# A multi-head attention block on one core: x transposed by DMA instead of by TensorE

## The chip, the cores and the metric

The kernel runs on one core of a Trainium2 chip. A core has five engines with queues of their own: TensorE (PE, with a row of its own in the profile for weight loads, PEld), VectorE (DVE), ScalarE (ACT), GpSimd (POOL) and SyncE (SP). Each engine executes its instructions in the order in which they stand in its queue; an instruction that has to wait holds up all that stand behind it. Transfers are issued from the queues of SP, ACT and POOL and are moved by 16 DMA engines that all queues share. The metric is the device time of one execution in microseconds (us).

## The reference

```
B, S, D, H = 1, 2048, 448, 16
qkv = (x @ wqkv).reshape(B, S, 3, H, 28).transpose(2, 0, 3, 1, 4)
scores = einsum("bhqd,bhkd->bhqk", q, k) * 28 ** -0.5
o = einsum("bhqk,bhkd->bhqd", softmax(scores), v)
out = o.transpose(0, 2, 1, 3).reshape(B, S, D) @ wo
```

All inputs and the output are bfloat16. x is 2048 x 448, wqkv is 448 x 1344, wo is 448 x 448.

## The kernel before, in words

The 16 heads are worked on in four groups of four (g = 0 to 3). A head of 28 numbers takes one of four bands of 32 partitions. The 2048 queries are cut into four chunks of 512 (c) and the 2048 keys into 16 tiles of 128. A pair of group and chunk is a set; there are 16 sets, one after another. Within a set, PE multiplies a tile of keys KA with a chunk of queries QP and leaves scores in PSUM. ACT takes most of them through the exponential (line 928, tiles of 128 x 1024, into `pt`). DVE does the others by an exponential of its own in integers (line 943, into `I`), of which shifted copies J are added by DVE (line 1014) or by an accumulating DMA that POOL issues (line 990). PE then multiplies pt, I and J with three scaled versions of V into bank `o` (line 1073). The sums are normalised (line 1123) and multiplied with WO.

K, Q and V are projections of x. A contraction runs over partitions, so PE needs x with its 448 columns on partitions: that is `XT`, for each of four blocks of 512 rows. The columns are cut in CC = 4 chunks of CK = 112, so that the weights lie as 112 x 4 x columns. x is loaded as it is (`load_x`, line 140, tiles `xs`): partition p gets rows 16p to 16p + 15, and block b takes the four of them from 4b on. `xt_job` transposes it: 16 PE transposes of 128 x 112 a block (line 621), half of them copied from PSUM into XT by ACT (line 629), half by DVE (line 627). Afterwards the xs tiles hold the normalised outputs. The rows of a block are therefore not neighbours in x, and the output is written with the same rearrangement (`out_perm`).

The start of the kernel is this. SP and ACT each issue half of x and one of the two small weight pieces of group 0 for K (tile `o_sb`, called G1) and for Q (tile `rr`, called G0); SP then issues the three full weights `WRAW` (W2 for V, W0 for Q, W1 for K). ACT loads its function table (line 160). PE runs ten matmuls on zeros (line 643), then transposes and projections. For group 0, `k_first` projects the keys of one block (line 298), ACT squares them (line 324), PE sums the squares over a head with `blockK` (line 409), DVE takes the maximum `kp` (line 414). When all four blocks have their maximum, DVE works out `kmt`, `kroot` and `su` (lines 418, 420, 496), which every score of the first set needs: su is the offset that keeps the exponential in range. `q_job` and `qn_first` do the same for the queries of chunk 0 (`z`, line 457, and the norm, line 487).

The operand QP has the queries and, in the free rows of a band, the offsets. SP fills constant rows by 16 small transfers (line 198, from a `pt` tile), then writes z (line 661) and su (line 502) into QP of chunk 0. Until that is there, a score is computed by two matmuls, one with z and one with su; the function `wide` decides which form is emitted.

The order on the engines is fixed when the kernel is built. A planner steps through time with a duration for every operation and takes, for each engine, the ready operation with the best priority; transfers from DRAM enter with a due time that is written down in a table (`evt[n] = (t, "DMA")`), which holds due times and isn't measured. It emits zero matmuls (line 762) where PE would otherwise stand still. On the chip the queues keep the planned order, and semaphores make each instruction wait until its data are there. Transfers share eight semaphores in turn: where a transfer takes one that an earlier transfer still holds, its issue waits until that one has landed.

Of the kernel before, what the change touches and what calls it, by code (L numbers as in the profile page):

```python
# [7 lines left out]
ACT = mybir.ActivationFunctionType  # L8
ALU = mybir.AluOpType
AX = mybir.AxisListType  # L10
BF16 = mybir.dt.bfloat16
# [28 lines left out]
def kernel(  # L40
# [7 lines left out]
    nc = tc.nc  # L48
    P = 128
    _, S, D = x.shape  # L50
    H = 16
    Dh = D // H
    HP = 32
    G = 4
    HG = 4
    CC = 4
    CK = D // CC
    QW = 512
    NQC = S // QW
    NKT = S // P  # L60
# [6 lines left out]
    WPAD = 4  # L67
    XB = 4
    NXB = NKT // XB
# [26 lines left out]

    x2 = x[0]
    out2 = out[0]
    out_perm = out2.rearrange("(p t) d -> p t d", t=NKT)

    const = ctx.enter_context(tc.tile_pool(name="const", bufs=1))
    big = ctx.enter_context(tc.tile_pool(name="big", bufs=1))
# [1 line left out]
    wk = ctx.enter_context(tc.tile_pool(name="wk", bufs=2))  # L104
    dram = ctx.enter_context(tc.tile_pool(name="dram", bufs=2, space=bass.MemoryType.DRAM))

    XT = [[big.tile([CK, CC // 2, QW], BF16, name=f"XT{b}_{k}") for k in range(2)] for b in range(NXB)]
    WRAW = [big.tile([CK, CC, D + WPAD], BF16, name=f"WRAW{t}") for t in range(3)]
    WG = [wk.tile([P, QW], F32, name=nm, bufs=n)[0:CK, 0:CC * (HG * Dh + WPAD) // 2].bitcast(BF16)
          .rearrange("p (c n) -> p c n", c=CC) for nm, n in (("rr", 1), ("o_sb", 2))]  # L110
    WO = big.tile([P, G, D], BF16, name="WO")
    VT = [None] * NTERM
    for k in range(NTERM):
# [4 lines left out]
        for b in range(NXB):  # L118
            t = big.tile([P, XB, G - GH, P], BF16, name=f"V{k}_{GH}_{b}")
            for g in range(GH, G):  # L120
                VT[k][g, b] = t[:, :, g - GH, :]
            VT[k][None, b] = t[:]
    xs = [big.tile([P, XB, D], BF16, name=f"xs{b}") for b in range(NXB)]
    QP = [[[big.tile([P, QW], BF16, name=f"QP{c}_{k}_{z}") for z in range(2)] for k in range(2)] for c in range(NQC)]
    OTL = [big.tile([P, QW], BF16, name=f"OTL{c}") for c in range(NQC)]

    def otile(g, c):
        if g < G - 1:
            return xs[c][:].rearrange("p t d -> p (t d)")[:, g * QW:(g + 1) * QW]
        return OTL[c][:]  # L130

    wq3 = wqkv.rearrange("(cc p) n -> p cc n", p=CK)
    x3 = x2.rearrange("(p t) c -> p t c", t=NKT)

    def load_w(t, eng):
        eng.dma_start(out=WRAW[t][:, :, 0:D], in_=wq3[:, :, t * D:(t + 1) * D])

    def load_x(b, eng, k=0, n=1):
        w = XB // n
        eng.dma_start(out=xs[b][:, k * w:(k + 1) * w, :], in_=x3[:, b * XB + k * w:b * XB + (k + 1) * w, :])  # L140

    def load_w0(t, eng):
        eng.dma_start(out=WG[t], in_=wq3[:, :, t * D:t * D + HG * Dh + WPAD])

    load_x(0, nc.sync, 0, 2)
    load_x(0, nc.scalar, 1, 2)
    for b in range(1, NXB):
        load_x(b, nc.sync, 0, 2)
        load_x(b, nc.scalar, 1, 2)
        if b == 1:  # L150
            load_w0(1, nc.sync)
            load_w0(0, nc.scalar)
    load_w(2, nc.sync)
    load_w(0, nc.sync)
    load_w(1, nc.sync)

    from concourse.hw_specs import get_activation_tables
    for idx, funcs in enumerate(get_activation_tables(nc.m.arch, ()).values()):
        if ACT.Exp in funcs and ACT.Identity in funcs:
            nc.scalar.add_instruction(mybir.InstLoadActFuncSet(  # L160
                name=nc.get_next_instruction_name(), act_func_set_id=idx, ins=[], outs=[]))
# [3 lines left out]
    ident = const.tile([P, P], BF16, name="ident")  # L165
# [16 lines left out]
    for i in range(HG):  # L182
        rows = slice(HP * i, HP * i + Dh)
# [18 lines left out]
                                base=-(HP * i + Dh + NQC - 1), pattern=[[0, 1]], channel_multiplier=1)  # L202
    for t in range(3):
        nc.gpsimd.memset(WRAW[t][:, :, D:D + WPAD], 0.0)

    def clear_v(g, b):
        v = VT[0][g, b]
# [9 lines left out]
    for h in range(H):  # L217
        g, i = divmod(h, HG)
# [11 lines left out]
    def bank_tile(tg):  # L230
        return psum.tile([P, QW], F32, name=tg, tag=tg, bufs=1)
# [8 lines left out]
    held = {}  # L240
# [52 lines left out]
    def mm_proj(ps, t, g, c, ccs):  # L293
        for cc in ccs:
            for i in range(HG):
                h = g * HG + i
                w = WG[t] if g == 0 else WRAW[t]
                nc.tensor.matmul(out=ps[HP * i:HP * (i + 1), :], lhsT=w[:, cc, h * Dh:h * Dh + HP],  # L298
                                 rhs=XT[c][cc // 2][:, cc % 2, :], start=(cc == 0), stop=(cc == CC - 1),
                                 tile_position=(0, HP * i))  # L300
# [240 lines left out]
    def v_job(g, b, t0, bank, pri, gate=0, eng="DVE"):  # L541
# [7 lines left out]
        def mm(part):  # L549
            if part == 0:  # L550
                held[key] = bank_tile(bank)
            for u in range(part * n // parts, (part + 1) * n // parts):
                for cc in range(CC):
                    quarters(held[key][:, u * w:(u + 1) * w], XT[b][cc // 2][:, cc % 2, (t0 + u) * P:(t0 + u + 1) * P],
                             WRAW[2][:, cc, g0 * HG * Dh:g1 * HG * Dh], cc == 0, cc == CC - 1)

        def evac():
# [51 lines left out]
        add("SP", 0.4, store, need=[key], gives=[key + ("st",)], pri=9, land=5.0)  # L609
        old.append(key + ("st",))  # L610


    def xt_job(b, banks, pri):
        def tr(hf):
            held[("xt", b, hf)] = bank_tile(banks[hf])
            v = held[("xt", b, hf)][:].bitcast(BF16)
            for c2 in range(CC // 2):
                for t in range(XB):
                    k = c2 * XB + t
                    cc = hf * CC // 2 + c2  # L620
                    nc.tensor.transpose(out=v[0:CK, k * P:(k + 1) * P],  # L621
                                        in_=xs[b][:, t, cc * CK:(cc + 1) * CK], identity=ident[:])

        def evac(hf):
            src = held.pop(("xt", b, hf))[:].bitcast(BF16)[0:CK, 0:2 * QW].rearrange("p (c q) -> p c q", c=2)
            if hf == 1:
                nc.vector.tensor_copy(out=XT[b][hf][:], in_=src)
            else:
                nc.scalar.copy(out=XT[b][hf][:], in_=src)

        for hf in range(2):
            add("PE", 0.5, lambda hf=hf: tr(hf), need=[("x", b)], gives=[("xt", b, hf)], acq=banks[hf], pri=pri + 0.01 * hf,
                cols=896)
            add("DVE" if hf else "ACT", 0.65 if hf else 0.97, lambda hf=hf: evac(hf), need=[("xt", b, hf)],
                gives=[("XT", b, hf)], rel=banks[hf], pri=pri)
# [745 lines left out]
```

## Time and profile before

| | |
|---|---|
| median of 3 runs | 361.59 us (361.31 to 361.6) |
| the profiled execution | 361.72 us, its span 359.9 us |
| PE busy | 343.1 us, 95% |
| DVE busy | 335.4 us, 93% |
| ACT busy | 341.1 us, 95% |
| POOL busy | 170.2 us, 47% |
| PE transposes of x (line 621) | first at 5.43 us, last group at 11.64 us |
| K projections of group 0 (line 298, bank a or d) | at 7.95, 9.96, 12.18 and 14.78 us |

A row of the groups has the line, the engine, the operation, the tiles written and read, their shapes and the count, then the busy time, the mean of one in ns, and the idle time before them with what ended it. A row of the timeline has the start, the duration, the engine, the line and the tiles; where several are merged, the count stands behind. "SPq" and "ACTq" are the issues of transfers in these queues. An idle engine costs time only where others wait for it.

### The profile page before, as it was taken

To read this page: it belongs to the slowest core of one execution; us is meant where nothing else is said; L and a number is where in the kernel's file an instruction comes from. 1 tells how busy PE (TensorE), PEld (TensorE's weight loads), DVE (VectorE), ACT (ScalarE), POOL (GpSimd) and SP (SyncE) were. 2 spreads that over 40 slices of the span, in tenths; PEclk is the share of its full clock that TensorE was granted. 3 is DMA by queue.
4 is the path that set the end of the run, shared out by engine and by line. 5 is a ranking of instruction groups with operands and counts; after the bars stand their busy time and mean duration, and the time that the engine had idled before them with its cause. 6 is when DMAs were issued, how large, how long until landed. Compare 5 with 4: busy or idle time off the path is not lost.

```text
span 359.9 us, 11256 instructions
## 1 busy us (share of the span) xinstructions
PE 343.1 (95%) x4520; PEld 111.3 (31%) x4521; DVE 335.4 (93%) x617; ACT 341.1 (95%) x373; POOL 170.2 (47%) x213
## 2 busy tenths in 40 slices
PE   8999999999999999999999999999889999999995
PEld 4533233332234322332232222222222222222233
DVE  8689999999989999999899999999999999999863
ACT  3789999999999999999999999999999999999991
POOL 8951353655444483545635765465546362521010
PEclk9999999999999999999999999999999999999999
DMA  8620063555636765365577646377857685672111
GB/s 242 142 47 15 21 125 86 113 107 105 135 75 129 148 124 113 89 132 108 117 143 149 120 91 137 78 152 158 177 116 156 128 176 129 142 147 66 34 51 54
DMA packets 24017, 41.17 MB, mean 114 GB/s; under 512 B 8604, under 2 KB 15004, under 8 KB 23964
## 3 DMA queue, kind: packets, MB, share of 16 engines
q0 software_dynamic: 8432, 29.24, 42.0%
q1 hardware_dynamic: 14348, 10.07, 10.3%
q10 hardware_dynamic: 1184, 1.14, 1.0%
q8 instruction: 35, 0.57, 0.6%
q14 instruction: 18, 0.15, 0.1%
HBM read 7.58 MB, written 1.96 MB: 27 GB/s over the span
## 4 chain that ended last, share of the span: by engine, by line
PE 37%; ACT 30%; DVE 23%; issue 9%; DMA 1%; DVEq 0%; ACTq 0%
ACT pt L928 30%; PE a L730 12%; DVE I L943 10%; PE o L1073 10%; PE m L305 5%; DVE J L1014 5%; PE m L298 4%; DVE V L579 2%; DVE V L566 2%; DVE KA L338 1%; PE o L643 1%; PE d L730 1%; DVE QA L460 1%; DVE o_sb L1100 1%; PE d L621 1%
## 5 line engine op out<-in xcount | busy, mean ns | idle before, releaser
L928 ACT ACTIVATE pt<-a 128x1024 bf16<-128x1024 f32 x358 | 329.7, 1129 | 2.9 <-PE a L730 1.3
L943 DVE TENSOR_SCALAR I<-d 128x512 int16<-128x512 f32 x278 | 181.0, 680 | 10.1 <-PE d L730 8.8
L730 PE MATMUL a<-QP,KA 32*128 32x512 bf16 (+1 forms) x704 | 137.3, 381 | 8.9 <-ACT pt L928 8.0
L1073 PE MATMUL o<-pt,V 128*32 128x512 bf16 x716 | 105.2, 384 | 0.0
L730 PE MATMUL d<-QP,KA 32*128 32x512 bf16 (+1 forms) x273 | 95.7, 383 | 0.8 <-DVE I L943 0.2
L730 PEld LDWEIGHTS <-KA 32*128 32x128 bf16 (+1 forms) x1041 | 46.1, 91 | 143.5 <-issue 141.7
L990 POOL DMA_DIRECT2D J<-I x55 | 49.6, 902 | 73.0 <-DVE I L943 49.6
L1073 PE MATMUL o<-J,V 128*32 128x512 bf16 x616 | 82.7, 384 | 0.0
L979 POOL MEMSET J<- 128x1024 int32 x55 | 60.1, 1094 | 36.7 <-PE d L730 12.0
L1014 DVE TENSOR_SCALAR J<-I 128x2048 int16<-128x2048 int16 x99 | 73.9, 764 | 0.6
L1073 PE MATMUL o<-I,V 128*32 128x512 bf16 x308 | 64.3, 384 | 0.1
L1073 PEld LDWEIGHTS <-V 128*32 128x32 bf16 x1640 | 30.8, 94 | 48.2 <-issue 45.1
L1123 POOL TENSOR_TENSOR xs<-o_sb,rr 128x512 bf16<-128x512 f32 x12 | 16.9, 1404 | 27.3 <-DVE J L1014 26.9
L298 PE MATMUL m<-XT,WRAW 112*32 112x512 bf16 x384 | 29.6, 384 | 0.2 <-DVE QA L460 0.2
L320 POOL TENSOR_TENSOR sq<-QA 128x512 bf16<-128x512 bf16 x15 | 16.8, 1122 | 23.1 <-DVE QA L460 17.8
L305 PE MATMUL m<-WRAW,XT 112*32 112x112 bf16 (+1 forms) x768 | 20.7, 230 | 0.3 <-DVE KA L338 0.3
L943 DVE TENSOR_SCALAR I<-m 128x512 int16<-128x512 f32 x30 | 20.3, 678 | 0.0
L320 POOL TENSOR_TENSOR sq<-KA 128x512 bf16<-128x512 bf16 x12 | 14.2, 1185 | 9.4 <-DVE J L1014 8.5
L305 PEld LDWEIGHTS <-XT 112*32 112x32 bf16 x768 | 12.3, 96 | 11.5 <-issue 11.4
L305 PE MATMUL m<-WO,xs 128*32 128x448 bf16 x156 | 12.5, 358 | 0.0
L730 PE MATMUL m<-QP,KA 32*128 32x512 bf16 (+1 forms) x30 | 11.5, 384 | 0.0
L460 DVE CAST QA<-m 128x512 bf16<-128x512 f32 x15 | 10.2, 683 | 0.7 <-PE m L298 0.7
(116 smaller groups left out, 207.3 us busy)
## 6 DMA issues: line engine op xcount, KB each, us to landing
J<-I POOLq DMA_DIRECT2D x55, 512.0 KB, 4.9
rr<-scr SPq DMA_DIRECT2D x60, 64.0 KB
QP<-QA SPq DMA_DIRECT2D x60, 28.0 KB
out_dram<-osb SPq DMA_DIRECT2D x12, 112.0 KB
WRAW<-in_wqkv_dram SPq DMA_DIRECT2D x3, 392.0 KB
xs<-in_x_dram ACTq DMA_DIRECT2D x4, 224.0 KB
xs<-in_x_dram SPq DMA_DIRECT2D x4, 224.0 KB
QP<-su SPq DMA_DIRECT2D x32, 2.0 KB
```

The lines of the kernel that those rows point to most:

```text
L298: nc.tensor.matmul(out=ps[HP * i:HP * (i + 1), :], lhsT=w[:, cc, h * Dh:h * Dh + HP], rhs=XT[c][cc // 2][:, cc % 2, :], start=(cc == 0), s ...
L305: nc.tensor.matmul(out=out[r, :], lhsT=lhsT[:, r], rhs=rhs, start=start, stop=stop, tile_position=(0, HP * i), **k)
L320: after_shared(nc.gpsimd.tensor_tensor(out=t[:], in0=src, in1=src, op=ALU.mult))
L460: nc.vector.tensor_copy(out=t[:], in_=held[key][:, 0:QW])
L730: nc.tensor.matmul(out=out_ap, lhsT=KAt[(g, j // XB)][r, (j % XB) * P:(j % XB + 1) * P], rhs=q[r, :], start=(n == 0), stop=(n == len(terms ...
L928: nc.scalar.activation(out=pt[:], in_=ps[:], func=ACT.Exp, scale=LN2 / 128.0)
L943: nc.vector.tensor_scalar(out=dst, in0=pd[:], scalar1=BIAS, scalar2=0.0, op0=ALU.add, op1=ALU.max)
L979: m = nc.gpsimd.memset(ch[1][:].bitcast(I32), fill)
L990: after_shared(nc.gpsimd.dma_start(out=ch[1][:, w], in_=ch["I"][:, w], accum_op=ALU.add))
L1014: cur["shared"] = nc.vector.tensor_scalar(out=r[:, w], in0=ch["I"][:, w], scalar1=float(SHIFT[k]), scalar2=None, op0=ALU.add)
L1073: nc.tensor.matmul(out=o[HP * i:HP * (i + 1), :], lhsT=VT[e["k"]][g, j // XB][:, j % XB, HP * i:HP * (i + 1)], rhs=e["ap"], start=(SETMM[k ...
L1123: m = nc.gpsimd.tensor_tensor(out=otile(g, c), in0=st["o_sb"][:], in1=st["rr"][:], op=ALU.mult)
```

## The change

x is no longer loaded and transposed on PE. For each block of 512 rows, SP issues two transposing transfers from DRAM: one writes columns 0 to 383 as three chunks of 128 into `XT` (128 x 3 x 512), the other writes columns 320 to 447 as one chunk of 128 into `XE` (128 x 1 x 512). Chunks are 128 rows long. The last one overlaps the third by 64 columns, so the first 64 rows of the weights' last chunk are set to zero, by DVE in G0 and G1 and by POOL in W0 to W2. Each weight is loaded by two transfers, and all ten are issued from ACT, ahead of its table load. Blocks now hold neighbouring rows, and the output is stored in the plain order. The table of due times is a new one, and the K copies of blocks 1 and 2 are no longer held back (`late`). xt_job goes, with its transposes and copies.

```diff
-    CK = D // CC
+    CK = P
+    CT = D - CK
...
-    out_perm = out2.rearrange("(p t) d -> p t d", t=NKT)
+    out_perm = out2.rearrange("(t p) d -> p t d", p=P)
...
-    XT = [[big.tile([CK, CC // 2, QW], BF16, name=f"XT{b}_{k}") for k in range(2)] for b in range(NXB)]
+    XT = [[big.tile([CK, CC - 1, QW], BF16, name=f"XT{b}"), big.tile([CK, 1, QW], BF16, name=f"XE{b}")] for b in range(NXB)]
...
-    xs = [big.tile([P, XB, D], BF16, name=f"xs{b}") for b in range(NXB)]
+    xs = [big.tile([P, (G - 1) * QW], BF16, name=f"xs{b}") for b in range(NXB)]
...
+    def xt(b, cc):
+        return XT[b][0][:, cc, :] if cc < CC - 1 else XT[b][1][:, 0, :]
...
-    load_x(0, nc.sync, 0, 2)
-    load_x(0, nc.scalar, 1, 2)
-    for b in range(1, NXB):
-        load_x(b, nc.sync, 0, 2)
-        load_x(b, nc.scalar, 1, 2)
-        if b == 1:
-            load_w0(1, nc.sync)
-            load_w0(0, nc.scalar)
-    load_w(2, nc.sync)
-    load_w(0, nc.sync)
-    load_w(1, nc.sync)
+    def load_w(t, eng, n=D):
+
+        dst = WG[t] if n < D else WRAW[t][:, :, 0:D]
+        cols = slice(t * D, t * D + n)
+        eng.dma_start(out=dst[:, 0:CC - 1, :], in_=wqkv[0:(CC - 1) * CK, cols].rearrange("(cc p) n -> p cc n", p=CK))
+        eng.dma_start(out=dst[CC * CK - D:CK, CC - 1, :], in_=wqkv[(CC - 1) * CK:D, cols])
+
+    def load_x(b):
+        rows = slice(b * QW, (b + 1) * QW)
+        nc.sync.dma_start_transpose(out=XT[b][0][:], in_=x2[rows, 0:(CC - 1) * CK])
+        nc.sync.dma_start_transpose(out=XT[b][1][:], in_=x2[rows, CT:D])
+
+    for t in range(2):
+        nc.vector.memset(WG[t][0:CC * CK - D, CC - 1, :], 0.0)
+    for t in (1, 0):
+        load_w(t, nc.scalar, HG * Dh + WPAD)
+    for b in range(NXB):
+        load_x(b)
+    for t in (2, 0, 1):
+        load_w(t, nc.scalar)
...
     for t in range(3):
         nc.gpsimd.memset(WRAW[t][:, :, D:D + WPAD], 0.0)
+        nc.gpsimd.memset(WRAW[t][0:CC * CK - D, CC - 1, 0:D], 0.0)
...
-                                 rhs=XT[c][cc // 2][:, cc % 2, :], start=(cc == 0), stop=(cc == CC - 1),
+                                 rhs=xt(c, cc), start=(cc == 0), stop=(cc == CC - 1),
...
-    def xt_job(b, banks, pri):
...
-    for n, t in (("x", 0), 4.9), (("G", 1), 6.9), (("G", 0), 6.9), (("x", 1), 6.2), (("x", 2), 8.0), (("x", 3), 9.3), \
-            (("W", 2), 10.9), (("W", 0), 12.0), (("W", 1), 13.2):
+    for n, t in [(("XT", k, h), 5.0 + 2.3 * k) for k in range(NXB) for h in range(2)] + \
+            [(("G", 1), 4.6), (("G", 0), 4.9), (("W", 2), 9.0), (("W", 0), 11.0), (("W", 1), 13.0)]:
         evt[n] = (t, "DMA")
...
-    for b in range(NXB):
-        xt_job(b, ("d0", "d1") if b % 2 == 0 else ("o", "m"), 1.0 * b)
     k_first(0, "a0", None, "DVE", "ACT", 1.5)
-    k_first(1, "a1", "o", "ACT", "ACT", 3.05, late=("ksq", 0, NQC - 1))
-    k_first(2, "d0", "a0", "ACT", "ACT", 3.1, late=("ksq", 0, NQC - 1))
+    k_first(1, "a1", "o", "ACT", "ACT", 3.05)
+    k_first(2, "d0", "a0", "ACT", "ACT", 3.1)
     k_first(3, "d1", "o", "DVE", "ACT", 3.2, late=("QA", 0, 0))
```

More of the change, by code (lines that the diff above doesn't have):

```diff
@@ L122 @@
             VT[k][None, b] = t[:]
-    xs = [big.tile([P, XB, D], BF16, name=f"xs{b}") for b in range(NXB)]
+    xs = [big.tile([P, (G - 1) * QW], BF16, name=f"xs{b}") for b in range(NXB)]
     QP = [[[big.tile([P, QW], BF16, name=f"QP{c}_{k}_{z}") for z in range(2)] for k in range(2)] for c in range(NQC)]
     OTL = [big.tile([P, QW], BF16, name=f"OTL{c}") for c in range(NQC)]
+    def xt(b, cc):
+        return XT[b][0][:, cc, :] if cc < CC - 1 else XT[b][1][:, 0, :]
     def otile(g, c):
         if g < G - 1:
-            return xs[c][:].rearrange("p t d -> p (t d)")[:, g * QW:(g + 1) * QW]
+            return xs[c][:, g * QW:(g + 1) * QW]
         return OTL[c][:]
[L132 to L143, printed above, removed]
-    load_x(0, nc.sync, 0, 2)
-    load_x(0, nc.scalar, 1, 2)
-    for b in range(1, NXB):
-        load_x(b, nc.sync, 0, 2)
-        load_x(b, nc.scalar, 1, 2)
-        if b == 1:
-            load_w0(1, nc.sync)
-            load_w0(0, nc.scalar)
-    load_w(2, nc.sync)
-    load_w(0, nc.sync)
-    load_w(1, nc.sync)
+    def load_w(t, eng, n=D):
[15 more added lines that the diff above has]
+        load_w(t, nc.scalar)
     from concourse.hw_specs import get_activation_tables
@@ L553, in mm @@
                 for cc in range(CC):
-                    quarters(held[key][:, u * w:(u + 1) * w], XT[b][cc // 2][:, cc % 2, (t0 + u) * P:(t0 + u + 1) * P],
+                    quarters(held[key][:, u * w:(u + 1) * w], xt(b, cc)[:, (t0 + u) * P:(t0 + u + 1) * P],
                              WRAW[2][:, cc, g0 * HG * Dh:g1 * HG * Dh], cc == 0, cc == CC - 1)
@@ L610, in oproj_job @@
         old.append(key + ("st",))
-    def xt_job(b, banks, pri):
[L614 to L635, printed above, removed]
-    for n, t in (("x", 0), 4.9), (("G", 1), 6.9), (("G", 0), 6.9), (("x", 1), 6.2), (("x", 2), 8.0), (("x", 3), 9.3), \
-            (("W", 2), 10.9), (("W", 0), 12.0), (("W", 1), 13.2):
+    for n, t in [(("XT", k, h), 5.0 + 2.3 * k) for k in range(NXB) for h in range(2)] + \
+            [(("G", 1), 4.6), (("G", 0), 4.9), (("W", 2), 9.0), (("W", 0), 11.0), (("W", 1), 13.0)]:
         evt[n] = (t, "DMA")
```

## The prediction

> **What bounds the kernel now.** I read the page first, for the share of each engine and the costliest groups, then the timeline of the first 25 us, because all the edits lie there, then the transfers in short windows. The page:
>
> ```profile
> span 359.9 us, 11256 instructions
> PE 343.1 (95%) x4520; PEld 111.3 (31%) x4521; DVE 335.4 (93%) x617; ACT 341.1 (95%) x373; POOL 170.2 (47%) x213
> ...
> L928 ACT ACTIVATE pt<-a 128x1024 bf16<-128x1024 f32 x358 | 329.7, 1129 | 2.9 <-PE a L730 1.3
> L943 DVE TENSOR_SCALAR I<-d 128x512 int16<-128x512 f32 x278 | 181.0, 680 | 10.1 <-PE d L730 8.8
> ```
>
> From the first exponential (19.39 us) on, ACT runs 358 exponentials, 329.7 / 358 = 0.92 us each, with 2.9 us idle in all; DVE and PE are as full. The changed kernel, as built, has 358 exponentials, 308 DVE conversions (278 and 30 from bank m here) and the same J additions too. So the main loop costs what it did, and the change is worth what it does to the start. That start is a chain of four K projections, each with a square (ACT), a norm matmul and a maximum (DVE); all four maxima are needed for the first score:
>
> ```profile
> 4.99 1.28 ACT L160 ACT_TABLE_LOAD   x1 [4.99 <-DMA xs<-in_x_dram]
> ...
> 7.63 11.51 SPq L198 DMA_DIRECT2D QP<-pt  x16
> ...
> 14.78 1.05 PE L298 MATMUL d<-XT,o_sb 112*32 112x512 bf16 x16
> ...
> 15.94 0.69 ACT L324 ACTIVATE sq<-d,kmask 128x512 bf16<-128x512 f32 x1 [0.67 <-PE d L298]
> ...
> 19.39 1.94 ACT L928 ACTIVATE pt<-a 128x1024 bf16<-128x1024 f32 x2 [0.68 <-PE a L730]
> ...
> 22.56 1.09 SPq L502 DMA_DIRECT2D QP<-su  x2
> ...
> 25.15 0.39 PE L730 MATMUL a<-QP,KA 32*128 32x512 bf16 x2
> ```
>
> To be seen: the last square starts at 15.94, the first exponential 3.45 us later. The first scores use two matmuls each (z and su) because QP0 isn't there; SP writes 16 fills, then z's rows, then su's, until 23.65, and the first score from QP0 runs at 25.15, after six double steps. Both are lines at which the change can lose.
>
> Three stretches of 1 us (a row has its bounds, its length, then the busy us of PE, PEld, DVE, ACT and POOL, PE's clock, the DMA share and GB/s), then the packets of two stretches, 4.4 to 5.8 us and 9.5 to 12.5 us:
>
> ```profile
> 2.00:3.00 1.00, 1.00 (x4) 0.42 (x3) 0.81 (x15) 0.00 (x0) 0.90 (x6) 1.00 0.79 122
> 3.00:4.00 1.00, 1.00 (x4) 0.32 (x3) 0.99 (x5) 0.00 (x0) 0.92 (x4) 1.00 1.03 384
> ...
> 12.00:13.00 1.00, 1.00 (x21) 0.45 (x18) 1.00 (x2) 0.65 (x1) 0.94 (x4) 1.00 1.10 251
> ```
>
> ```profile
> DMA packets 998, 0.43 MB, mean 310 GB/s; under 512 B 861, under 2 KB 998, under 8 KB 998
> ...
> q10 hardware_dynamic: 481, 0.25, 63.7%
> q1 hardware_dynamic: 517, 0.18, 53.9%
> ```
>
> ```profile
> DMA packets 859, 0.74 MB, mean 247 GB/s; under 512 B 32, under 2 KB 859, under 8 KB 859
> ```
>
> The 16 DMA engines are full from 2.5 to 13.5 us. Packet prices: at 384 GB/s the 1792-byte packets of x take 16 x 1792 / 384 = 75 ns of one engine. In the 1.4 us of the second fence 137 such packets take 10.2 of 22.4 engine-us; the 861 packets of 232 bytes share 12.2, 14 ns each (by the queues' shares, 117.6%, it is 19). The 896-byte packets of the weights: 48 / 859 = 56 ns.
>
> **What is removed.** 64 PE transposes (16 take 1.69 us, later eights 0.61), four ACT copies of 1.0 and four DVE copies of 0.67 us. All lie before 13.2 us. ACT and DVE have gaps between them there, so the gain isn't their sum: it is only how much earlier the K chain can run, and that is set by what now replaces them.
>
> **What is added: eight transposing transfers.** No row shows one. They read x as 512 x 3 and 512 x 1 pieces of 256 bytes per pair, 8192 in all, 512 per engine. Bounds: at 384 GB/s a piece takes 10.7 ns, 5.5 us in all; from above, if blocks of 128 x 128 (64 of them, 32 KB) went one after another, each like a WO transfer (24.5 KB lands 2.0 us after its issue), 128 us. I take 16 ns, between 14 and 19, since the 232-byte packets are nearest in size: 8.2 us.
>
> **The queues, in order.** ACT now issues all ten weight transfers ahead of its table load; SP the transposes. A semaphore is shared by every eighth transfer, and the next one on it waits until the earlier has landed. In the built order, ACT's second W2 part waits for the first G1 part, W0's for G0 and for XE0, W1's for XT1 and W2; then comes the table load. SP: XE1 waits for XT0, XT3 for W2, XE3 for XE1, and the eighth fill of QP waits for XE3.
>
> When has XT1 landed? First data at about 2.0; per engine 224 pieces x 16 ns = 3.6; G, 56 packets at 16 ns, 0.9; W2, 28 at 56 ns, 1.6; of W0's 1.6, which starts near 5 us and alternates with the pieces, I count 1.0; last packet to semaphore 0.7 (a WO transfer's 2.0 less the 1.3 between first issue, 0.74, and first data): 9.8 us.
>
> From there ACT: two issues of 0.45, table load 1.28, so the first square (K0) begins at +2.25, where before the table was ready at 6.27 and hid behind x. Then, by the built order and the rows' durations: square 0.69, DVE KA0 0.81, z 0.80, kp 0.69 (+5.35); only then PE's norm of Q may overwrite that bank, and K2's projection stands behind it in PE's order (+5.65 to 6.7), square +6.8 to 7.5, norm, K3's projection +7.8, its square +9.0, which is 18.8 us against 15.94. The first exponential keeps its 3.45 behind: 22.25, **2.9 us later**. The planner, whose order this is, puts XT1 at 7.3 and knows of no wait on ACT; its numbers are inputs, not measurements.
>
> XE3 lands at 2.0 + 8.2 + 0.9 + W2 and W0 (56 packets, 3.1) + half of W1 (0.8) + 0.7 = 15.7, under the 17.6 at which PE asks for it. But behind it: the eighth fill 0.5, eight fills 4.0, z's rows 3.3, su's 1.1, landing 1.5, so QP0 stands at 15.7 + 10.4 = 26.1. The built order uses it after four double steps, not six: 26.1 - 25.15 + 2 x 0.92 = **2.8 us later**. The two paths run beside each other; I count the longer, 2.9.
>
> By a rule that I weigh here: Advanced Engine Details and Errata (X-Bar Transpose) in the Trainium skill gives transposing transfers 350 to 400 GB/s, about as fast as plain ones; at 375 the 0.92 MB up to XT1 would take 2.4 us instead of 3.6, and the loss would be 1.7 us. No run here shows it.
>
> **Edits at nothing.** Contraction over 128 rows instead of 112: a 512-column matmul lasts 0.38 us with 112 rows and with 128. Two small DVE memsets (0.06 each) stand ahead of zero: 0.1 us, covered by the wait for x. Three POOL memsets of 64x448, about 0.45 each, push WO's loads from 22.4 to 23.8 us; they are needed by PE only many tens of us later; uncovered, 1.4. The plainer row order of the output makes the last 1792-byte packets two of 896: 112 instead of 75 ns each, under 0.3 us at the end, or nothing.
>
> Sum: the profiled execution took 361.72 us (its span 359.9 and 1.8 around it), 0.13 over the median of 361.59. 361.59 + 2.9 = **364.5 us**.
>
> **Rivals.**
> *Faster: the transposes are cheap and ACT is free early.* Place: the landing of XT1. If pieces take 10.7 ns and the weights fill gaps only, XT1 lands at 2.0 + 2.4 + 0.6 + 0.7 = 5.7, the first exponential comes at 5.7 + 12.45 = 18.15, 1.2 us earlier: 360.4. It decides below XT1 = 6.9 us. For it: 384 GB/s in one row. Against: the 232-byte packets ran well below that rate, and W2 is queued ahead of the pieces' end. Between XT1 = 6.2 and 7.7 us nothing measurable changes.
> *Transposes at half the rate of plain packets*, 32 ns a piece, because a 256-byte row has to be spread over 128 partitions. XE3: 2.0 + 16.4 + 0.9 + 4.7 + 0.7 = 24.7; QP0 at 35.1; 35.1 - 25.15 + 1.84 = 11.8 later: 373.4. Nothing in the trace speaks against it but the absence of the operation.
> *Blocks one after another.* XE3 at 2 + 128 us, so some 117 us later: near 479. Against it: 16 engines otherwise share every transfer. VectorE: DVE Perf Modes (The three transpose paths) in the Trainium skill advises TensorE for 128x128 where PSUM will do, with 390 ns against 1309 by DMA; 64 x 1.309 = 84 us would be a loss of about 73, an estimate by that page.
> *PE falls to half clock.* The warm-up shows it: ten 512-column matmuls take 4.45 us, 0.43 each, later ones 0.21. With waits of 2.7 us between projections the new start could run so, adding 1.0 for each of K2 and K3: 366.5. It widens the likeliest case.
>
> **How the numbers follow.** Change within 0.2% (0.72 us) is what a measurement of this kernel can't tell from none. Likeliest, 1 to 6 us later: 0.60, own range 362.6 to 367.5. Half rate: 0.15. One after another: 0.05. Faster: 0.13. Same: 0.07. Faster 0.13, same 0.07, slower 0.80. The range leaves out the slowest rival (0.05) and most of the faster one (0.08): 361.0 to 374.0.
>
> **What would show it.** Right: table load after 10 us and named as waiting for an XT transfer; first exponential at 21 to 23.5; first score from QP0 near 26; 0.92 us per exponential as before. Wrong: XT1's projection before 7 us (faster), XT3's after 20 (half rate), or a main loop whose ACT gaps grow or shrink by over 1 us, since the planner reorders all of it and I price that at nothing.

## The result, and the profile after

The changed kernel takes 370.98 us in the median (370.36 to 372.29, 4 runs), against 361.53 for the kernel before on the same chip: a ratio of 1.0267, with a 95% interval of 1.0238 to 1.0297. It is 9.5 us slower, where 2.9 were forecast. The profiled execution is the longest of the four, 372.29 us with a span of 370.5; the others have spans of 368.6 to 369.5.

The page of the changed kernel shows the main loop at the durations that it had, and more idle time ahead of the same 358 exponentials:

```profile
span 370.5 us, 11130 instructions
PE 344.6 (93%) x4457; PEld 108.4 (29%) x4457; DVE 335.1 (90%) x615; ACT 337.5 (91%) x369; POOL 171.0 (46%) x216
...
L902 ACT ACTIVATE pt<-a 128x1024 bf16<-128x1024 f32 x358 | 330.2, 1140 | 7.4 <-PE d L704 5.0
L917 DVE TENSOR_SCALAR I<-d 128x512 int16<-128x512 f32 x278 | 180.8, 679 | 12.6 <-PE d L704 11.3
```

330.2 us of exponentials answer to 329.7, and 180.8 us of conversions to 181.0. ACT's idle time ahead of its exponentials grew from 2.9 to 7.4 us, DVE's from 10.1 to 12.6. The loss lies in waits, and most of it at the start. From the timeline of the changed kernel's first 31 us (start, duration, engine, line, tiles), first ACT and PE:

```profile
10.79 0.37 ACTq L140 DMA_DIRECT2D WRAW<-in_wqkv_dram  x1
...
11.20 0.51 ACTq L141 DMA_DIRECT2D WRAW<-in_wqkv_dram  x1
...
11.74 1.28 ACT L160 ACT_TABLE_LOAD   x1 [11.74 <-DMA WRAW<-in_wqkv_dram]
...
13.04 0.69 ACT L325 ACTIVATE sq<-a,kmask 128x512 bf16<-128x512 f32 x1
...
16.84 1.47 PE L299 MATMUL d<-XT,o_sb 128*32 128x512 bf16 x12
...
19.74 0.83 PE L299 MATMUL d<-XT,o_sb 128*32 128x512 bf16 x12
...
20.90 0.69 ACT L325 ACTIVATE sq<-d,kmask 128x512 bf16<-128x512 f32 x1 [0.85 <-PE d L299]
...
24.34 1.94 ACT L902 ACTIVATE pt<-a 128x1024 bf16<-128x1024 f32 x2 [0.71 <-PE a L704]
...
30.21 0.49 PE L704 MATMUL a<-QP,KA 32*128 32x512 bf16 x2 [2.17 <-DMA QP<-su]
```

Then SP alone, without a gap in the list:

```profile
0.74 1.40 SPq L145 DMA_TRANSPOSE XT<-in_x_dram  x1
2.19 1.26 SPq L146 DMA_TRANSPOSE XE<-in_x_dram  x1
3.49 1.70 SPq L145 DMA_TRANSPOSE XT<-in_x_dram  x1
5.23 2.02 SPq L146 DMA_TRANSPOSE XE<-in_x_dram  x1
7.30 2.48 SPq L145 DMA_TRANSPOSE XT<-in_x_dram  x1
9.83 2.34 SPq L146 DMA_TRANSPOSE XE<-in_x_dram  x1
12.21 1.51 SPq L145 DMA_TRANSPOSE XT<-in_x_dram  x1
13.77 1.30 SPq L146 DMA_TRANSPOSE XE<-in_x_dram  x1
15.18 8.89 SPq L198 DMA_DIRECT2D QP<-pt  x16
24.17 3.67 SPq L635 DMA_DIRECT2D QP<-z  x4
27.95 1.09 SPq L503 DMA_DIRECT2D QP<-su  x2
```

Two things are to be seen. ACT's issue of W1 stands until 10.79, which is when XT1 has landed; the profile names a WRAW transfer at the table load, the last one ahead of it in the queue. And SP is occupied by the eight transposing transfers from 0.74 to 15.07 us: issuing them takes 14.0 us together. Only then can it start on the sixteen fills, z's rows and su's, and PE waits for su until 30.21.

The lag is the start of the nth exponential less that of the same one before (the first: 24.34 - 19.39 = 4.95). It can be read off both traces for every one of the 358, and shows where the time goes. The trace is that of the longest execution, so its 10.6 us at the end of the span are 1.1 more than the 9.5 between the medians; no trace shows which entry is smaller in the others.

| exponential | lag, us | what is late there |
|---|---|---|
| 1st | 4.95 | the K chain: table load behind XT1 |
| 5th | 7.06 | QP of chunk 0 isn't written |
| 9th | 8.12 | PE at half clock after that wait |
| 100th | 8.08 | nothing |
| 200th | 8.34 | a single addition of J, 0.28 |
| 276th | 9.95 | two slow additions of J near the 261st, 1.6 in all |
| last | 10.00 | nothing |
| end of the span | 10.6 | the end, 0.6 |

The third row is in the windows of the changed kernel (bounds, length, busy us of PE, PEld, DVE, ACT and POOL, PE's clock, DMA share, GB/s):

```profile
29.00:30.00 1.00, 0.00 (x0) 0.00 (x0) 0.00 (x0) 0.00 (x0) 0.00 (x0) 1.00 0.01 4
...
32.00:33.00 1.00, 1.00 (x23) 0.25 (x15) 0.79 (x2) 0.85 (x2) 0.00 (x0) 0.53 0.00 0
33.00:34.00 1.00, 1.00 (x23) 0.38 (x16) 0.99 (x2) 1.00 (x1) 0.00 (x0) 0.50 0.06 16
```

PE, which had no matmul from 28.04 to 30.21, comes back at full clock and drops to half at 32.07, about two microseconds later; the trace's record of the clock has it back at full at 35.48, 3.41 us after the drop.

### The profile page after: what moved, and what is told of

Its sections match the earlier page's. It is cut to its first block, busy times and chain, and to the rows that moved or that the text cites. A ratio compares the mean times of both kernels' runs of the same rounds, so it can differ in the third digit from the quotient of the medians.

```text
span 370.5 us, 11130 instructions
## 1 busy us (share of the span) xinstructions
PE 344.6 (93%) x4457; PEld 108.4 (29%) x4457; DVE 335.1 (90%) x615; ACT 337.5 (91%) x369; POOL 171.0 (46%) x216
## 4 chain that ended last, share of the span: by engine, by line
PE 39%; ACT 25%; DVE 23%; issue 9%; DMA 2%; SPq 1%; ACTq 0%; DVEq 0%
ACT pt L902 25%; PE a L704 14%; PE o L1047 11%; DVE I L917 10%; DVE J L988 5%; PE m L306 5%; PE m L299 4%; DMA XT<-in_x_dram 2%; DVE V L580 2%; DVE V L567 2%; PE d L704 1%; DVE KA L339 1%; DVE QA L461 1%; PE d L299 1%; DVE o_sb L1074 1%
## 5 line engine op out<-in xcount | busy, mean ns | idle before, releaser
L902 ACT ACTIVATE pt<-a 128x1024 bf16<-128x1024 f32 x358 | 330.2, 1140 | 7.4 <-PE d L704 5.0
L917 DVE TENSOR_SCALAR I<-d 128x512 int16<-128x512 f32 x278 | 180.8, 679 | 12.6 <-PE d L704 11.3
L704 PE MATMUL a<-QP,KA 32*128 32x512 bf16 (+1 forms) x708 | 138.7, 383 | 11.1 <-ACT pt L902 7.9
L704 PE MATMUL d<-QP,KA 32*128 32x512 bf16 (+1 forms) x275 | 97.0, 385 | 1.1 <-DVE I L917 0.5
L988 DVE TENSOR_SCALAR J<-I 128x2048 int16<-128x2048 int16 x99 | 75.7, 782 | 0.6
L1047 PE MATMUL o<-I,V 128*32 128x512 bf16 x308 | 65.1, 386 | 0.2 <-DVE I L917 0.2
L299 PE MATMUL m<-XT,WRAW 128*32 128x512 bf16 x288 | 24.4, 386 | 0.2 <-DVE QA L461 0.2
L306 PE MATMUL m<-WRAW,XT 128*32 128x112 bf16 (+1 forms) x576 | 17.9, 233 | 0.3 <-DVE KA L339 0.3
L306 PEld LDWEIGHTS <-XT 128*32 128x32 bf16 x576 | 9.4, 96 | 11.5 <-issue 11.4
L306 PE MATMUL m<-WRAW,XE 128*32 128x112 bf16 (+1 forms) x192 | 11.6, 230 | 0.0
```

What stands on the lines that cost most here:

```text
L704: nc.tensor.matmul(out=out_ap, lhsT=KAt[(g, j // XB)][r, (j % XB) * P:(j % XB + 1) * P], rhs=q[r, :], start=(n == 0), stop=(n == len(terms ...
L902: nc.scalar.activation(out=pt[:], in_=ps[:], func=ACT.Exp, scale=LN2 / 128.0)
L917: nc.vector.tensor_scalar(out=dst, in0=pd[:], scalar1=BIAS, scalar2=0.0, op0=ALU.add, op1=ALU.max)
L988: cur["shared"] = nc.vector.tensor_scalar(out=r[:, w], in0=ch["I"][:, w], scalar1=float(SHIFT[k]), scalar2=None, op0=ALU.add)
L1047: nc.tensor.matmul(out=o[HP * i:HP * (i + 1), :], lhsT=VT[e["k"]][g, j // XB][:, j % XB, HP * i:HP * (i + 1)], rhs=e["ap"], start=(SETMM[k ...
```

## The experiments

My theory, formed from these rows: two paths end late, ACT's (XT1, table load, squares) and SP's (transposes, fills, su), and the later of the two counts; the half clock follows from the wait. The rivals: the transposing transfers are slow in themselves; the large weights take the DMA engines from them; the contraction over 128 rows costs time in the main loop.

### ACT's path taken away (e1)

W0 and W1 are issued by POOL, behind its clearing of V, near 13.5 us.

```diff
-    for t in (2, 0, 1):
-        load_w(t, nc.scalar)
+    load_w(2, nc.scalar)
...
+    for t in (0, 1):
+        load_w(t, nc.gpsimd)
```

> W0 and W1 are issued by POOL after its V clears instead of by ACT, so nothing on ACT waits for XT1. Theory (two lines: the table load behind XT1's landing, and QP0 behind the transposes and 16 fills): table load done before 6 us, first square near 7, first exponential 20.5 to 22.5 instead of 24.34, set now by the last transposes; but the first score from QP0 stays at 29.5 to 30.5, so the time moves little, 369.5 to 371. Rival A (the landing of the last transposes alone sets the start): first exponential stays above 23.8. Rival B (a single line, the start, and what is saved there is saved at the end): 368 to 369.

371.21 us (370.12 to 371.93), ratio 1.0265 (95% interval, in square brackets from here on: [1.0244, 1.0286]): no better than the change, and 0.2 above the expected range, though the timeline of this kernel starts almost as early as before:

```profile
4.29 1.28 ACT L159 ACT_TABLE_LOAD   x1 [4.29 <-issue]
...
13.68 8.89 SPq L197 DMA_DIRECT2D QP<-pt  x16
...
19.70 1.94 ACT L903 ACTIVATE pt<-a 128x1024 bf16<-128x1024 f32 x2 [0.74 <-PE a L705]
...
26.01 1.09 SPq L504 DMA_DIRECT2D QP<-su  x2
...
28.17 0.68 PE L705 MATMUL a<-QP,KA 32*128 32x512 bf16 x2 [4.78 <-DMA QP<-su]
```

The first exponential lags by 0.31 us, the fifth by 5.22: four double steps are done early and PE then stands for 4.78 us. With the first path out of the way, SP's path sets the time.

### SP's path shortened (e2), and both (e3)

The eight fills of QP with z = 1, which the first set doesn't read, go to POOL; e3 does this and e1's edit.

```diff
-    for z in range(2):
+    for z in range(1):
         for c in range(NQC):
             for k in range(2):
                 nc.sync.dma_start(out=QP[c][k][z][HP * k + Dh + NQC - 1 - c:P:2 * HP, :], in_=offs)
...
+    for z in range(1, 2):
+        for c in range(NQC):
+            for k in range(2):
+                nc.gpsimd.dma_start(out=QP[c][k][z][HP * k + Dh + NQC - 1 - c:P:2 * HP, :], in_=offs)
```

> The eight fills of the second set of QP buffers are issued by POOL, so SP reaches z's rows eight fills (some 4 us) earlier. Theory: first exponential unchanged at 24.3, first score from QP0 without a wait (QP0 ready by 26.5), no fall of PE's clock after it; gain of 2.1 (the wait) and about 1.0 (half clock): 367.5 to 368.5. Rival A (the landing of the last transposes is all) and a rival that puts the loss into the reordered main loop: under 0.7 us of gain.

> Both moves together. Theory: first exponential 20.5 to 22.5, first score from QP0 near 26 with at most 1 us of wait; 364.5 to 366.5. If the two lines were one, the gain would be that of the better of the two alone.

e2: 368.29 us (367.74 to 368.82), 1.0188 [1.0171, 1.0205]. Its timeline has no wait for QP left, and seven exponentials run on without a gap:

```profile
23.73 1.09 SPq L507 DMA_DIRECT2D QP<-su  x2
...
24.07 1.94 ACT L906 ACTIVATE pt<-a 128x1024 bf16<-128x1024 f32 x2 [0.76 <-PE a L708]
...
26.20 6.75 ACT L906 ACTIVATE pt<-a 128x1024 bf16<-128x1024 f32 x7 [0.19 <-PE d L708]
```

The lag stays at the 4.4 us of the K chain. e3: 364.87 us (364.69 to 365.08), 1.0093 [1.0078, 1.0108]; first exponential at 19.94, lag 0.55, then 1.2 to 1.5 until the slow additions near the 261st, which add 1.62, and 3.15 at the end. With one path gone the other sets the time; with both gone two thirds of the loss are gone.

The same move of the fills in the kernel before (e4):

> The kernel before with the eight fills of the second QP set issued by POOL. Theory: in the kernel before, QP0 came just in time, so moving fills gives nothing there: 361.0 to 362.0, first exponential 19.4, sixth step unchanged. Rival (the fills always cost): faster by over 1 us.

362.06 us (361.66 to 363.53), 1.0020 [1.0009, 1.0032]. That is 0.06 above what was expected and no gain: the fills were no burden to the kernel before; their place matters only behind the transposes.

### PE kept busy through the wait (e5)

```diff
+        if wide(items[0][1][0], t) and "kept" not in held:
+            held["kept"] = True
+            kept = bank_tile("o")
+            for _ in range(10):
+                nc.tensor.matmul(out=kept[:], lhsT=zero[:, 0:P], rhs=zero[:], start=True, stop=True)
```

> Ten zero matmuls (2.1 us at full clock) stand in PE's queue ahead of the first score from QP0, in the time in which PE waits. Theory: the wait itself stays (first score from QP0 near 30), but the clock of 0.50 at 32 to 35 us goes, and with it about 1.0 us (the exponentials 5 to 8 fall 1.1 us further behind in the changed kernel): 369.5 to 370.2. Rival: the drift has another cause, time unchanged or longer.

368.71 us (368.3 to 369.03), 1.0198 [1.0183, 1.0213]. The windows of the same stretch, with the zero matmuls in it:

```profile
29.00:30.00 1.00, 1.00 (x7) 0.29 (x5) 0.00 (x0) 0.00 (x0) 0.00 (x0) 1.00 0.01 2
...
32.00:33.00 1.00, 1.00 (x30) 0.45 (x31) 1.00 (x3) 1.00 (x2) 0.00 (x0) 1.00 0.00 0
```

The wait for QP stays (lag 6.53 at the fifth exponential), the half clock doesn't come, and the lag is 6.28 at the ninth instead of 8.12. So the half clock is caused by PE's idleness: between the fifth and the ninth exponential the lag grows by 1.06 us with it and shrinks by 0.25 without it, so it costs 1.1 to 1.3. The gain of 2.3 us between the medians is more than expected. Between the two traces it is 3.8 (spans of 370.5 and 366.7), with two further parts: the first exponential came 0.6 us earlier, and the slow additions near the 261st, 1.6, are absent. The page TensorE: Matmul & The Clock Gate in the Trainium skill (Part 1) puts the drop after an idle window of about 3.4 us; here PE had stood for 2.17 us and was busy for 0.94 to 1.00 of each of the four microseconds from 24 to 28 us, so the drop needed no 3.4 us without any matmul.

### Fewer, larger transposes (e6, e8)

Four transposing transfers of 1024 rows in place of eight of 512; e8 adds both edits of e3.

```diff
-    XT = [[big.tile([CK, CC - 1, QW], BF16, name=f"XT{b}"), big.tile([CK, 1, QW], BF16, name=f"XE{b}")] for b in range(NXB)]
+    XT = [[big.tile([CK, CC - 1, 2 * QW], BF16, name=f"XT{b}"), big.tile([CK, 1, 2 * QW], BF16, name=f"XE{b}")] for b in range(NXB // 2)]
...
-        rows = slice(b * QW, (b + 1) * QW)
+        rows = slice(2 * b * QW, 2 * (b + 1) * QW)
```

> The eight transposing transfers become four, of twice the rows (1024 rows each); the same pieces move, all else is as in the changed kernel. Theory (each transposing transfer costs SP 1.25 to 1.4 us of issue whatever its size, more where the DMA engines are full, and that paces them): SP is done issuing before 11 us instead of 15.1, the last one lands by 14 us instead of 17.5; first projection later (both blocks must land); first exponential 19.5 to 23, first score from QP0 near 26; 365 to 368. Rival (issue goes with the number of pieces, or the pieces' own time paces them): issue still ends near 15 us, the last lands near 17, time 369 to 371.5.

> Four transposing transfers, W0 and W1 from POOL, the second set of fills from POOL. Theory: all three lines are eased at once; first exponential 17.5 to 20, no wait for QP0; 360.5 to 363.5, the lower end only if the slow J addition near the 261st exponential, which the traces of the changed kernel and of three variants show (1.85 us instead of 0.76), stays away. Rival (transposing transfers are slower than the chain on PE in any arrangement): first exponential above 20.5, time above 364.

e6: 367.55 us (367.1 to 368.81), 1.0169 [1.0149, 1.0189]. SP's timeline there:

```profile
0.74 3.31 SPq L146 DMA_TRANSPOSE XT<-in_x_dram  x1
4.10 1.29 SPq L147 DMA_TRANSPOSE XE<-in_x_dram  x1
5.43 4.69 SPq L146 DMA_TRANSPOSE XT<-in_x_dram  x1
10.17 1.30 SPq L147 DMA_TRANSPOSE XE<-in_x_dram  x1
```

10.6 us of issuing instead of 14.0: neither a fixed price per transfer, which would have halved it, nor a price per piece, which would have kept it. A transfer of 512 pieces takes 1.24 us at best and one of 1024 1.28; one of 1536 takes 1.34 at best (e9, e12, e14), one of 3072 3.31. SP is through at 11.47 us, and the lag falls to 3.5. e8 is 366.16 us (365.11 to 369.43), 1.0155 [1.0105, 1.0205], no better than e3 and outside the expected 360.5 to 363.5: its first exponential starts at 21.20 instead of 19.94. That a block of 1024 rows lands later, which no longer pays once SP's path is out of the way, is my reading of it; no run separates it.

### The contraction alone (e7)

The kernel before, with chunks of 128 rows and PE's transposes as they were.

```diff
-    CK = D // CC
+    CK = P
...
-                                        in_=xs[b][:, t, cc * CK:(cc + 1) * CK], identity=ident[:])
+                                        in_=xs[b][:, t, min(cc * CK, CT):min(cc * CK, CT) + CK], identity=ident[:])
```

> The kernel before with the contraction in chunks of 128 rows alone: PE transposes 128 columns at a time (the last chunk overlaps), weights in two transfers each, zeros for the overlap; x is still loaded as it is. Theory: the wider contraction costs nothing in PE; only the five further transfers on SP and ACT (some 0.45 us each) shift the start: within 0.7 us of before, 361.2 to 362.2. Rival (128 rows cost PE or its clock something in the main loop): above 362.5.

362.49 us (362.35 to 362.7), 1.0026 [1.0016, 1.0035], between the theory's 362.2 and the rival's 362.5. The lag is 0.67 at the first exponential, at most 1.26 between, 0.69 at the last one, and 0.94 at the end of the span. This edit costs 0.9 us in the kernel before. Two thirds of it are there at the first exponential and the rest comes behind the last, so the main loop has no lasting share; which of the start's instructions it is, no run separates.

### Which part is ACT's wait, which the weights' share (e10, e11, e13)

e1 moved two large weights, so it took away ACT's wait and also their packets among the transposed pieces. e10 was to keep the packets and drop the wait, by issuing W0 and W1 from POOL near 4 us; e11 issues only W1 from POOL, late; e13 is e1 with a small transfer that makes ACT wait for XT1 again:

```diff
+    probe = const.tile([1, 64], BF16, name="probe")
+    nc.scalar.dma_start(out=probe[:], in_=XT[1][0][0:1, 0, 0:64])
```

> The changed kernel with W0 and W1 issued by POOL as early as it can (near 4 us, before its V clears), so the weights still share the DMA engines with the transposes, but ACT waits for nothing. Theory (ACT's wait for XT1's landing ahead of the table load is what delays the first squares): first square near 7, first exponential 20 to 22 instead of 24.34. Rival (it was the weights' share of the DMA engines, which the variant with late W0 and W1 took away): first exponential above 23. In both the first score from QP0 stays late, 28 to 30.5, and the time 369 to 371.5.

> The changed kernel with W1 alone moved to POOL, behind its V clears; W2 and W0 stay on ACT where they were and share the DMA engines with the transposes as before. Theory (ACT's wait for XT1's landing, which W1's issue carries, delays the squares): ACT waits only for XE0, table load near 7.1 us instead of 11.74, first square near 8.4 instead of 13.04, first exponential 19.7 to 21.5; the score from QP0 stays near 29 and the time 369.5 to 371. Rival (the weights' share of the DMA engines): first exponential above 23.

> The kernel of e1 (W0 and W1 issued late, from POOL), with one transfer of 128 bytes out of XT1 put on ACT's queue ahead of the table load: ACT waits again for XT1's landing, but no large weight besides W2 shares the DMA engines with the transposes. Theory (ACT's wait for XT1 makes the late start of the changed kernel): table load after 10 us, first square near 12, first exponential at 22.5 to 24 instead of 19.70 in e1. Rival (the weights' share of the DMA engines makes most of it, and the wait alone is worth about the 0.9 us by which e11 was ahead of the changed kernel): first exponential at 19.9 to 21.0. The time moves little in either case, as QP0 is late in e1 too: 370 to 373.

e10 took 379.73 us (376.61 to 381.06), 1.0514 [1.0475, 1.0553], far outside the 369 to 371.5 of both expectations; its first exponential is at 28.31, on the rival's side of 23, but for a reason that neither named. SP's timeline shows where it stands:

```profile
7.38 8.70 SPq L145 DMA_TRANSPOSE XT<-in_x_dram  x1
```

and one of its windows (columns as above), whose last number is GB/s, how little is moved meanwhile:

```profile
10.00:11.00 1.00, 0.00 (x0) 0.00 (x0) 0.00 (x0) 0.00 (x0) 0.88 (x4) 1.00 0.91 106
```

The weights issued from POOL come in packets of 3584 and 4480 bytes, and beside them the transposed pieces nearly stand: 106 GB/s for both together, some 800 pieces from 8 to 14 us against 3300 in the changed kernel, and SP's issue of XT2 takes 8.70 us. The run says nothing on ACT's wait.

e11: 372.90 us (372.87 to 373.24), 1.0314 [1.0298, 1.0329]. ACT is free early, its first square is at 8.08, but K1's is at 13.68 all the same, now behind its data (the projection of K1 waits for XE1 until 13.01, in e1 it ran at 10.37), and the first exponential at 23.43, lag 4.04. I read from this that the weights' share was most of the loss, ACT's wait 0.9 of it. e13 corrects that: 371.45 us (370.4 to 371.61), 1.0265 [1.0251, 1.0279], and its timeline on ACT is

```profile
10.37 0.60 ACTq L156 DMA_DIRECT2D probe<-XT  x1
10.99 1.28 ACT L161 ACT_TABLE_LOAD   x1 [10.99 <-DMA XT<-in_x_dram]
12.29 0.69 ACT L328 ACTIVATE sq<-a,kmask 128x512 bf16<-128x512 f32 x1
...
23.35 1.94 ACT L905 ACTIVATE pt<-a 128x1024 bf16<-128x1024 f32 x2 [0.65 <-PE a L707]
```

Without any large weight but W2 beside the pieces, the wait alone makes the first exponential 3.96 us late. The wait without the share costs 3.65 more than e1 (23.35 - 19.70), the share without the wait 3.73 (23.43 - 19.70), both 4.64. They are two lanes side by side into the same chain of squares, and each alone is enough; neither can be called the larger part.

### Towards a version without the loss (e9, e12, e14)

e9 is e3 with W2, too, on POOL, near 9 us; e12 has the table load right behind the small weights, W2 on ACT after Q's square, only the two fills of chunk 0 that come first on SP, the other fourteen on POOL and W0 and W1 behind them; e14 puts those fourteen on SP behind chunk 0's su, where SP has nothing to do. The first edit below is in e12 and e14, the second in e14:

```diff
+        if key == ("Q", 0, 0):
+            load_w(2, nc.scalar)
...
+            for z in range(2):
+                for c in range(1 - z, NQC):
+                    for k in range(2):
+                        fill(nc.sync, c, k, z)
```

> As the variant with W0, W1 and the second fills on POOL, and W2 goes to POOL too, after its first eight V clears (near 9 us), so that the transposing transfers have the DMA engines nearly to themselves up to there. Theory (the issue of a transposing transfer costs 1.25 to 1.4 us on an idle DMA and more on a busy one, and paces them): issues end near 11.8 us instead of 13.8, the last pieces by 14 us, first exponential 18.3 to 19.3 instead of 19.94, wait for QP0 under 1 us; 361.3 to 364.3, the upper part if the slow J addition near the 261st exponential comes. Rival (the weights don't matter to the transposes): issues as long as with W2 in front, first exponential 19.7 to 20.1.

> The best order that I can make of these parts: the table load right behind the two small weights, W2 from ACT behind the square of Q, of the fills only chunk 0's on SP, the other 14 and then W0 and W1 on POOL behind the V clears, where no transpose is left to disturb. Theory: transposes issue end near 12 us, first exponential 18.5 to 19.6, no wait for QP0; 360.7 to 362.3, or up to 364 with the slow J addition. Rival (transposes by DMA can't be faster at the start than PE's in any order): first exponential at 19.8 or later, 362.5 or more.

> The kernel of e12, with the 14 fills that POOL issued moved to SP, behind su of chunk 0 (a source tile of their own), and W0 and W1 on POOL behind the clearing of WO, so that POOL's queue is free some 8 us earlier. Theory (what was left of the loss in e12 is POOL's queue, through which the square of QA1 and so QP1 came late): the lag of 3.7 us at exponentials 15 to 20 goes; first exponential near 19.5, lag -0.3 to 0.5 there, end 0 to 2 depending on the slow additions: 361.3 to 363.3. Rival (the transposing transfers cost the main loop something of their own): the lag comes back at the same place without POOL's queue in the way, 364.5 to 366.

e9: 367.17 us (366.56 to 367.5), 1.0153 [1.0137, 1.0168], where 361.3 to 364.3 was expected. SP's issues became shorter (12.2 us in all), but beside W2's packets from POOL only 27 pieces were moved between 11 and 12 us, where the microsecond ahead had 743, and the first exponential came at 21.21, later than in e3.

e12: 365.98 us (365.6 to 366.99), 1.0117 [1.01, 1.0134], 2 us above what was expected at most. The first exponential is at 19.55 and the sixth 0.29 us ahead of the kernel before. Then 3.7 us are lost between the 16th and the 21st. The timeline there:

```profile
26.37 9.08 POOL L225 DMA_DIRECT2D WO<-in_wo_dram  x16
...
36.02 1.03 POOL L326 TENSOR_TENSOR sq<-QA 128x512 bf16<-128x512 bf16 x1
...
37.11 0.62 PE L311 MATMUL m<-sq,maskK 128*32 128x512 bf16 x4 [2.59 <-POOL sq L326]
```

The square of the next chunk's queries stands behind fourteen fills, two weights and WO in POOL's queue. e14 frees that queue, and its POOL timeline has the square at its time:

```profile
30.90 1.04 POOL L322 TENSOR_TENSOR sq<-QA 128x512 bf16<-128x512 bf16 x1 [1.76 <-DVE QA L464]
```

The lag there is 0.64 to 0.97, which bears the reading out. e14 takes 364.8 us (363.72 to 367.23), 1.0094 [1.0066, 1.0121]. That is above the expected 361.3 to 363.3 and in the range of the rival, but the rival's sign, the lag coming back at that place, is absent. The first exponential is at 20.40, 0.85 later than in e12, and the last one of the profiled execution 2.89 behind: 0.8 is there ahead of the slow additions, which add 1.7 near the 261st exponential and 0.8 at 318 us, and some 0.3 is regained between. No version ran faster than the kernel before.

### The slow additions

In twelve of the thirteen kernels that load x by transposing transfers (all but e5) an addition of J near the 261st exponential takes 1.84 to 1.87 us, against a median of 0.68; before, e4 and e7 don't have it there. That is one traced execution of each; whether the others of the same kernel have it isn't known. The timelines of DVE and POOL in the changed kernel:

```profile
266.38 1.26 POOL L1097 TENSOR_TENSOR xs<-o_sb,rr 128x512 bf16<-128x512 f32 x1 [2.56 <-DVE I L917]
266.78 3.19 DVE L988 TENSOR_SCALAR J<-I 128x2048 int16<-128x2048 int16 x2
267.59 0.86 POOL L964 DMA_DIRECT2D J<-I  x1
268.31 1.11 POOL L953 MEMSET J<- 128x1024 int32 x1
```

and in the kernel before:

```profile
255.20 1.58 POOL L1123 TENSOR_TENSOR xs<-o_sb,rr 128x512 bf16<-128x512 f32 x1
...
257.01 0.87 POOL L990 DMA_DIRECT2D J<-I  x1 [0.23 <-POOL xs L1123]
...
258.44 1.56 DVE L1014 TENSOR_SCALAR J<-I 128x2048 int16<-128x2048 int16 x2
```

POOL's normalising product should start at 255.20 + 8.34 = 263.5, as its neighbours do, and starts at 266.38. The profile puts its wait down to `I`, but the product also reads `rr`, which SP fetches from DRAM in four transfers after having stored `rec` there, and the landings in the trace show what it waits for. From store to first fetch it is 4.9 us before and in e4, 4.7 in e7 and 4.6 in e5, and 6.2 to 6.5 in the twelve others. In the changed kernel the four fetches, issued by 261.09, then meet an accumulating transfer of J that POOL issued at 259.12, and the last two land only at 265.92 and 266.21; before, all four had landed by 252.74.

So the product falls beside the two additions, which take 3.19 us instead of 1.56. The same shows in e4 at another place: there the product waits 4.10 us for `rr`, starts at 116.67, 2.4 later than before, and falls beside two scaling operations on V, which take 2.70 us instead of 1.20; the lag grows by 1.1 us behind them. Advanced Engine Details and Errata (VectorE Performance Modes) in the Trainium skill says that a two-port mode of VectorE and GpSimd's instructions block each other, which agrees with 1.56 and 3.19; that the additions run in such a mode no row says, and no run moves the product alone. Why the stretch from store to fetch has two lengths isn't shown: the order of instructions on SP is the same in e5 and in the changed kernel.

## Why the prediction was wrong in its size

The direction was right and the time lies in the range, but the likeliest case, 364.5 us with its own 362.6 to 367.5, was 6.5 us short. By its own steps:

- **The second path is the step that failed: "XE3 lands at ... 15.7 ... so QP0 stands at 15.7 + 10.4 = 26.1".** It stood at 30.2. The sum took SP to be free for the first seven fills while the pieces were moving, so it priced SP's issue of eight transposing transfers at nothing. They take 14.0 us, back to back. All sixteen fills come after 15.18: 8.89 us, 3.67 for z, 1.09 for su, and the landing. The landing of XE3, from which the sum starts, bound nothing: the last piece of x had moved by 16.75, and SP came to the eighth fill only at 19.4. By the prediction's own rule the path is then 30.21 - 25.15 + 1.84 = 6.9 late, not 2.8; 7.06 was measured. Against the 2.9 that I counted, this is the largest term of the miss, 4.1 us; e2 takes the wait away, and with it 2.7 us of the time, since the first path then sets it.
- **"The two paths run beside each other; I count the longer"** was right. e1 removes the first path and the time doesn't move; e2 shortens the second and the first sets the time; only e3 gains from both.
- **The first path: right in mechanism, 2.1 us short.** XT1 landed at 10.8 instead of 9.8 (1.0). The first square came 2.25 behind it, exactly as summed, and the first exponential 3.44 after the last square (3.45 forecast). The squares between took 7.86 instead of 6.75 (1.1): PE's clock is 0.50 from 11.6 to 18.4 us, and 0.8 of the 1.1 is seen in the projection of K2, which takes 1.81 us from 16.84 on where that of K3, at full clock, takes 1.05. This is the rival of which I wrote that it "widens the likeliest case". It came true with about half of the 2.0 us that I gave it, and belonged in the sum.
- **The price of a piece, 16 ns between 14 and 19**, was right where pieces move alone: in e1 from 10 to 11 us they reach 274 GB/s, which is 15 ns of one engine for each. (The median record lasts 18 ns, but records of one engine overlap: the DMA share of that microsecond is 1.24.) The whole stream beside the weights lasts from 2.23 to 16.75 us: 2.1 MB in 14.5 us, 145 GB/s. The rival of half rate (32 ns) gave 373.4 us, close to the result, but by a mechanism that didn't happen. The 350 to 400 GB/s of Advanced Engine Details and Errata (X-Bar Transpose) in the Trainium skill aren't reached here, even by pieces alone.
- **"The main loop costs what it did"** was off by 3 us of the profiled execution: 1.06 for the half clock after QP's wait, which a late first path alone wouldn't have brought (e2 has none), 0.28 and 1.6 for the additions of J. The sign that I named, ACT's gaps growing by more than 1 us, is there: 2.9 to 7.4, though most of that is the wait for QP.
- **Edits at nothing.** The contraction, with its two transfers for each weight, costs 0.9 us by e7 in the kernel before; its share in the changed kernel, whose start is another, isn't separated. The end is 0.6 later in the profiled execution and 0 to 0.5 in the traces of the experiments on the changed kernel, where the form of the output may have a share; that was not tried alone.
- **The faster rival** was decided by XT1 below 6.9 us; it landed at 10.8. Even with ACT free early (e1, e3, e12) no first exponential came before 19.55.

## What to carry to other kernels

Price the queue that issues a transfer apart from the transfer: eight transposing transfers held SP for 14 us, and what stood behind them in that queue paid for it. Where two paths end at the same consumer, compute both to the end with the issue times in, since shortening one gains nothing until the other is shortened too. Count a wait of PE with what follows it: here one of 2.17 us was followed by 3.41 us of half clock, which cost another 1.1 to 1.3.

## What the runs showed of the hardware that I had not expected

- Issuing a transposing transfer takes at least 1.24 us on SP, nearly the same for 512 and 1024 pieces (1.28); 1.34 at best for 1536 and 3.31 for 3072; beside weights up to 2.5 in the changed kernel, 3.60 in e11 and 8.70 in e10. A fill of QP takes 0.56.
- Weights in POOL's packets of 3584 and 4480 bytes and the transposing stream together moved 106 to 151 GB/s in each microsecond from 8 to 14 us (e10); with the same weights issued from ACT in packets of 896 bytes, the changed kernel moved 172 to 320 there. Whether the packets' size or POOL's queue makes the difference, no run separates.
- PE's clock fell to 0.50 after a wait of 2.17 us, for 3.41 us, and ten zero matmuls in that wait kept it at 1.00.
